# Second expert's first product by seven block products, and the first expert cut at 576 and 240 rows

## Chip, cores and metric

One core of one Trainium2 chip. The metric is the device time of one execution in microseconds; lower is better. Three runs of the kernel before took 835.76, 841.76 and 845.5 us, median 841.76.

## What is computed

A block-sparse attention (4 sequences of 768 rows, 8 heads of 64) feeds a mixture of 8 experts. Each of the 3072 rows of 512 numbers goes to its two best experts; the part that matters here is the second half:

```
logits = x @ w_gate
noisy_logits = logits + np.log1p(np.exp(x @ w_noise)) * noise
top2 = np.argpartition(-noisy_logits, 2, axis=1)[:, :2]
...
for e in range(E):
    for k in range(2):
        mask = top2[:, k] == e
        h = np.maximum(x[mask] @ w1[e], 0.0)          # 512 -> 1024
        out[mask] += top2_w[mask, k, None] * (h @ w2[e])   # 1024 -> 512
```

## The kernel before

**Stages.** The attention runs first, in steps. Behind it a router (class `Router`) handles the rows in four groups of 768: a row's logits, its two experts, its place in each expert's list, and a table `tab` of row numbers and weights, built on TensorE from one-hot matrices in two halves per group (L758) and added up by VectorE (L761). The last group's routing runs beside the first expert's work.

**Units.** The experts are worked as nine units (`Experts.units`, L780). Expert 0 has two: unit 0 holds its rows of the first three groups, up to `CA` = 640, and unit 1 its rows of the last group, up to `CB` = 224. So unit 0 can start before the last routing is done. Units 2 to 8 are experts 1 to 7 with up to `C` = 816 rows each. Rows over these limits go to a slow loop behind the kernel (`overflow`).

**One unit.** GpSimd gathers the rows from DRAM into `xg` (`gather`, L978; a block of 128 rows each), SyncE's queue transposes them into `xta` or `xtb` (`xpose`, L994). The first product (w1) gives 1024 hidden numbers per row in eight groups `f` of 128. Every number is carried as a high and a low half-precision part, so each product is three matmuls. ScalarE writes the high part `hh` of the hidden numbers (`relu`, L1052), VectorE the low part `hl` (L1054). The second product (`mm2`) goes block by block of 128 rows: 24 matmuls of 512 columns (L1160). A remainder of up to 64 rows is done in 12 pairs that sit side by side in the array (L1170), a larger one in transposed form (L1179, then L1191). `finish` weights the rows, and GpSimd scatters them to the output (L1236).

**Plain and fast units.** With `u < FAST` = 3 a unit takes the plain first product: per group 4 x 3 matmuls for each of one or two stretches of rows (`part`, L1040). From unit 3 on it is `fast1`: seven block products in place of eight, each of 6 matmuls of 408 columns (L1079), for each of four pairs of groups. For it the weights are first combined by `sums` (splits L891/L892, sums L911) into the tile `wop`, and the rows by `halves` (L934 on VectorE, L952 on ScalarE) into the tile `tx`; `halves` works in the memory of `xg`, so the next unit's gathers wait for it. The helper `coming` spreads this work over the second product of the unit before.

**Order.** The program is written out in the order of issue and each engine keeps that order. The hooks are: `turn` (up to 20 steps of the router's generator; a step that yields 1 or 2 ends the call, and `FENCE` says how many later calls it then skips), `after(f)` behind each group of a first product, and the loop over blocks of a second product. `third()` is the generator that issues the gathers and transposes of units 1 and 2 once the last routing is done. Its steps are taken behind the blocks of unit 0 and in unit 1.

Of the kernel before, what the change touches and what calls it, by code (L numbers as in the profile page):

```python
# [18 lines left out]
P = 128  # L19
# [8 lines left out]
E = 8  # L28
C = 816
CA = 640  # L30
CB = 224
# [480 lines left out]
class Router:  # L512
# [96 lines left out]
    def run(self, b, ps):  # L609
# [50 lines left out]
        if last:  # L660
            nc.vector.tensor_copy(self.R[:, E:], self.R[:, 0:1])
            nc.vector.memset(self.R[:, 0:1], 0.0)
# [31 lines left out]
        ve = ef  # L694
        if last:
            ve = tile([P, T, 2], F32, "ve")
            nc.vector.scalar_tensor_tensor(ve, z0, float(E), ef, op0=ALU.mult, op1=ALU.add)
        cap = tile([P, T, 2], F32, "cap")
        nc.vector.tensor_scalar(cap, z0, float((CB if last else CA) - C), float(C), op0=ALU.mult, op1=ALU.add)
# [39 lines left out]
        for t in range(0, T, G):  # L739
# [23 lines left out]
            yield  # L763
        if last:
            left = C % P
            w = self.tab.rearrange("p (u c) v -> p u c v", c=NC)[:, 1:E, NC - 1, 1]
            nc.vector.tensor_copy(w[P // 2:P // 2 + left], w[0:left])


class Experts:  # L770
    def __init__(self, tc, router, w1, w2, out, x_dram, table):
# [10 lines left out]
        self.FAST = 3  # L782
# [25 lines left out]
    def open_rows(self, ctx):  # L808
        self.xp = ctx.enter_context(self.tc.tile_pool(name="mxp", bufs=1))
        self.xg = self.xp.tile([P, 7, 2 * self.D], F16, name="xg")  # L810
        self.nc.gpsimd.memset(self.xg[:, C // P], 0.0)
# [22 lines left out]

    def open_third(self, ctx):
        self.ps_h = [self.ps_h[0]] * 2 + [ctx.enter_context(self.tc.tile_pool(name="ps_h3", bufs=1, space=PSUM))]

# [26 lines left out]
    def open_first(self, e):  # L864
        KB, F = self.KB, self.F
        n = KB * F
        if e == 0:
            h, l = (self.wpa.tile([P, n], F16, name=x) for x in ("w1ha", "w1la"))
        else:
            both = self.sums_tile()  # L870
            h, l = both[:, 0:n], both[:, n:2 * n]
        view = lambda t: t.rearrange("p (k f) -> p k f", k=KB)
        self.wb[e] = {"w1h": view(h), "w1l": view(l)}
# [115 lines left out]
    def xpose(self, u, c):  # L989
        r = self.st["u", u]  # L990
        if c == 0:
# [202 lines left out]
    def finish(self, u, c, py, halves=False):  # L1194
# [6 lines left out]
        if u < 2:  # L1201
            nc.vector.tensor_scalar(y[0:m], py[0:m, 0:D], w[0:m, c:c + 1], None, op0=ALU.mult)
        elif u < len(self.units) - 1:
# [122 lines left out]
def count_overflow(nc, router, ps):  # L1326
# [5 lines left out]
    for sl, cap in ((slice(0, 1), CB), (slice(1, E), C), (slice(E, NV), CA)):  # L1332
# [9 lines left out]
def kernel(ctx, tc, q, k, v, v_windows, sampled_blocks, w_gate, w_noise, noise, w1, w2, out):  # L1342
# [154 lines left out]
    def third():  # L1497
# [7 lines left out]
        yield  # L1505
        for i in range(ex.count(1)):
            ex.xpose(1, i)
        for i in range(ex.count(1)):
            ex.gather(2, i)
        yield  # L1510
        for i in range(ex.count(2)):
            ex.xpose(2, i)
        yield

    def coming(u, k):
        e = ex.units[u][1]
        if u + 1 < ex.FAST:
            return
# [25 lines left out]
    for u in range(nu):  # L1544
        if u == 2:
            turns.close()
            ex.open_third(hidden)
        if u == ex.FAST:
# [8 lines left out]
        def after(f):  # L1557
# [7 lines left out]
            if u == 2 and f < 4:  # L1565
                ex.split_piece(e, 4 + f)
# [122 lines left out]
```

## Time and profile before

| what | value |
|---|---|
| median of three runs | 841.76 us |
| profiled execution | 835.04 us |
| its span, first to last instruction | 833.2 us |
| TensorE (PE) busy | 778.8 us, 93% |
| VectorE (DVE), ScalarE (ACT), GpSimd (POOL) busy | 523.5, 391.8, 365.9 us |

Stretches of the span, us from its start, cut where TensorE goes from one product to the next: attention to 301.5; unit 0 first product 301.5 to 333.0, second 333.0 to 360.4; unit 1 360.4 to 380.5; unit 2 first product 380.5 to 413.5, second to 447.5; unit 3 first product 447.5 to 476.5. Matmul rows overlap in time, since their ends are modelled; the time from one start to the next is what a matmul costs. In brackets a row shows how long its engine had stood idle and what ended that.

### The profile page before, as it was taken

To read this page: it belongs to the slowest core of one execution; us is meant where nothing else is said; L and a number is where in the kernel's file an instruction comes from. 1 tells how busy PE (TensorE), PEld (TensorE's weight loads), DVE (VectorE), ACT (ScalarE), POOL (GpSimd) and SP (SyncE) were. 2 spreads that over 40 slices of the span, in tenths; PEclk is the share of its full clock that TensorE was granted. 3 is DMA by queue.
4 is the path that set the end of the run, shared out by engine and by line. 5 is a ranking of instruction groups with operands and counts; after the bars stand their busy time and mean duration, and the time that the engine had idled before them with its cause. 6 is when DMAs were issued, how large, how long until landed. Compare 5 with 4: busy or idle time off the path is not lost. (4 is left out here: it accounts for less than half of the span.)

```text
span 833.2 us, 21747 instructions
## 1 busy us (share of the span) xinstructions
PE 778.8 (93%) x8889; PEld 475.5 (57%) x8889; DVE 523.5 (63%) x1024; ACT 391.8 (47%) x742; POOL 365.9 (44%) x552
## 2 busy tenths in 40 slices
PE   5899988988997898999999999999999999999996
PEld 3577767766676676475545545545545545545542
DVE  4454457557466557423376796796777787886831
ACT  4677666655674652212235445445445445445400
POOL 3465554430364500334055454555447547546521
PEclk9999998999999989999999999999999999999999
DMA  8968987881569789395944984984994894794311
GB/s 332 348 201 266 295 258 225 326 279 53 159 200 249 172 242 346 104 215 137 245 97 80 199 253 76 210 242 82 156 237 113 176 248 105 163 259 109 101 55 53
DMA packets 125707, 159.70 MB, mean 192 GB/s; under 512 B 66629, under 2 KB 84037, under 8 KB 125600
## 3 DMA queue, kind: packets, MB, share of 16 engines
q1 hardware_dynamic: 97232, 75.83, 33.6%
q0 software_dynamic: 20016, 57.47, 27.2%
q10 hardware_dynamic: 8352, 24.93, 9.5%
q8 instruction: 72, 1.18, 0.6%
q14 instruction: 35, 0.29, 0.1%
HBM read 117.30 MB, written 27.10 MB: 173 GB/s over the span
## 5 line engine op out<-in xcount | busy, mean ns | idle before, releaser
L1079 PEld LDWEIGHTS <-wop 128*128 128x128 f16 x1008 | 98.6, 98 | 76.7 <-issue 0.5
L1210 POOL DMA_INDIRECT pv<-out_dram,gi x42 | 96.6, 2301 | 96.2 <-ACT pv L1204 48.0
L1160 PEld LDWEIGHTS <-hh 128*128 128x128 f16 x768 | 74.6, 98 | 89.7 <-issue 2.5
L232 PE MATMUL s<-kv,q 64*32 64x192 f32 (+3 forms) x1920 | 86.8, 348 | 13.9 <-DMA kv<-in_k_dram 5.8
L324 ACT ACTIVATE t<-t 128x512 f32<-128x512 f32 (+1 forms) x120 | 63.1, 567 | 73.4 <-PE t L322 64.4
L1236 POOL DMA_INDIRECT out_dram<-pv,mt x42 | 56.9, 1355 | 84.3 <-DMA out_dram<-pv,mt 33.3
L1079 PE MATMUL mb<-tx,wop 128*128 128x408 f16 x432 | 83.5, 336 | 0.2 <-DVE us L1100 0.2
L322 PE MATMUL t<-r_ident,p 128*128 128x128 f32 x448 | 69.6, 295 | 9.4 <-ACT t L324 4.4
L267 DVE TENSOR_REDUCE nm<-s 128x4 f32<-128x1024 f32 (+1 forms) x48 | 54.3, 1131 | 36.2 <-PE s L232 20.8
L222 POOL COPY kv<-kv 128x128 f32 x264 | 69.6, 308 | 15.5 <-DMA kv<-in_k_dram 9.3
L1160 PE MATMUL py<-w2h,hh 128*128 128x512 f16 x192 | 72.8, 379 | 0.0
L1160 PE MATMUL py<-w1ha,hh 128*128 128x512 f16 x192 | 72.8, 379 | 0.0
L1160 PE MATMUL py<-w2l,hh 128*128 128x512 f16 x192 | 72.8, 379 | 0.0
L1160 PE MATMUL py<-w1la,hh 128*128 128x512 f16 x192 | 72.8, 379 | 0.0
L322 PEld LDWEIGHTS t<-r_ident,p 128*128 128x128 f32 x448 | 50.0, 146 | 35.9 <-issue 15.7
L310 ACT ACTIVATE p<-s,nb 128x256 f32<-128x256 f32 x176 | 69.4, 474 | 1.6
L978 POOL DMA_INDIRECT xg<-x_rows,gi x56 | 61.3, 1094 | 19.5 <-issue 15.9
L1160 PE MATMUL py<-w1ha,hl 128*128 128x512 f16 x192 | 68.9, 379 | 0.0
L1160 PE MATMUL py<-w2h,hl 128*128 128x512 f16 x192 | 68.8, 379 | 0.0
L1084 ACT ACTIVATE hh<-us 128x408 f16<-128x408 f32 x48 | 26.1, 543 | 89.1 <-DVE us L1100 82.5
L232 PEld LDWEIGHTS s<-kv,q 64*32 64x32 f32 (+2 forms) x1920 | 49.2, 126 | 30.4 <-issue 12.6
L1160 PEld LDWEIGHTS <-hl 128*128 128x128 f16 x384 | 37.6, 98 | 45.3
(214 smaller groups left out, 1457.9 us busy)
## 6 DMA issues: line engine op xcount, KB each, us to landing
wraw<-in_moe_w_dram SPq DMA_DIRECT2D x62, 512.0 KB
vb<-in_v_windows_dram ACTq DMA_DIRECT2D x28, 390.0 KB
vb<-in_v_windows_dram ACTq DMA_DIRECT2D x14, 520.0 KB
kv<-in_v_dram SPq DMA_DIRECT2D x4, 1560.0 KB
out_dram<-zero ACTq DMA_DIRECT2D x8, 768.0 KB
q<-in_q_dram SPq DMA_DIRECT2D x11, 512.0 KB
kv<-in_k_dram SPq DMA_DIRECT2D x7, 768.0 KB
x_rows<-x SPq DMA_DIRECT2D x20, 256.0 KB
```

The costliest lines, as they stand in the source:

```text
L222: nc.gpsimd.tensor_copy(KG[:, j, :, 32 * s:32 * s + 32], KT[:, :, bass.ds(offs[3 * j + s], 32)])
L232: mm = lambda out, l, r, pos: nc.tensor.matmul(out, l, r, start=True, stop=True, tile_position=pos)
L267: red = lambda out, x: nc.vector.tensor_reduce(out, x, axis=AX.X, op=ALU.max, negate=True)
L310: self.nc.scalar.activation(p[:, 256 * u:256 * u + 256], S[:, a, 256 * r:256 * r + 256], AF.Exp, bias=nb[:, u:u + 1], scale=0.125)
L322: self.nc.tensor.transpose(T[i][:, c:c + P], p[:, i * w + c:i * w + c + P], self.ident)
L324: self.nc.scalar.activation(t[:, i * w:(i + 1) * w], T[i][:, 0:w], AF.Copy)
L978: g = nc.gpsimd.indirect_dma_start(out=self.xg[0:m, c], out_offset=None, in_=self.x_dram[0:nr], in_offset=bass.IndirectOffsetOnAxis(ap=r[" ...
L1079: self.nc.tensor.matmul(bank[:, 0:H], w[:, h, o, k, cs], x(k, a), start=start and i == 0, stop=i == len(seq) - 1, skip_group_check=True)
L1084: self.nc.scalar.activation(self.hh[:, f, o], x, AF.Relu)
L1160: nc.tensor.matmul(py, h[:, f, o], w[x][:, f, :], start=i == 0, stop=i == last)
L1210: g = nc.gpsimd.indirect_dma_start(out=y[0:m], out_offset=None, in_=self.out, in_offset=bass.IndirectOffsetOnAxis(ap=r["gi"][0:m, c:c + 1] ...
L1236: x = self.nc.gpsimd.indirect_dma_start(out=self.out, out_offset=bass.IndirectOffsetOnAxis(ap=self.st["u", u]["mt"][0:m, c:c + 1], axis=0) ...
```

## The change

Four things. Unit 2 (expert 1) moves from the plain first product to `fast1` (`FAST` 3 to 2); its combined weights are made beside unit 0's second product, its combined rows beside unit 1. Expert 0 is cut at 576 and 240 rows, and rows of the first three groups beyond 576 are passed on to unit 1: for that, five small VectorE instructions join each of the first three routings. Unit 0 then ends in a remainder of 64 rows, done in pairs. The second half of the last table sum goes from the middle of unit 0's second product to the end of its first, and the gathers and transposes of units 1 and 2 are issued from the middle of the first block on. With the reference's inputs expert 0 has 575 rows in the first three groups and 202 in the last.

```diff
-CA = 640
-CB = 224
+CA = 576
+CB = C - CA
...
         cap = tile([P, T, 2], F32, "cap")
-        nc.vector.tensor_scalar(cap, z0, float((CB if last else CA) - C), float(C), op0=ALU.mult, op1=ALU.add)
+        if not last:
+            nc.vector.scalar_tensor_tensor(z0, pos, float(CA), z0, op0=ALU.is_ge, op1=ALU.mult)
+            more = cap[:, 0, 0:1]
+            nc.vector.tensor_reduce(more, z0.rearrange("p t k -> p (t k)"), axis=AX.X, op=ALU.add)
+            yield
+            nc.vector.scalar_tensor_tensor(pos, z0, float(-CA), pos, op0=ALU.mult, op1=ALU.add)
+            nc.vector.tensor_tensor(self.R[:, E:], self.R[:, E:], more, op=ALU.add)
+            yield
+        ve = tile([P, T, 2], F32, "ve")
+        nc.vector.scalar_tensor_tensor(ve, z0, float(E), ef, op0=ALU.mult, op1=ALU.add)
+        nc.vector.tensor_scalar(cap, z0, float(CB - C), float(C), op0=ALU.mult, op1=ALU.add)
...
-        self.FAST = 3
+        self.FAST = 2
...
+            if u == 1:
+                for i in {5: (0,), 6: (1,), 7: (2, 3)}.get(f, ()):
+                    ex.halves(2, i)
-            if u == 2 and f < 4:
-                ex.split_piece(e, 4 + f)
+            if u == 2 and f % 2 == 0:
+                ex.split_piece(e, 4 + f // 2)
...
-                    ex.mm1_first(f, (lambda: turn_rows(NS + 200), lambda: new_logits(NS + 300))[f] if f < 2 else None)
+                    if f == ex.FB - 1:
+                        FENCE[:] = [1, 1]
+                    ex.mm1_first(f, {0: lambda: turn_rows(NS + 200), 1: lambda: new_logits(NS + 300),
+                                     ex.FB - 1: turn}.get(f))
...
+        parts = [(s, i) for s in range(2) for i in range(4)]
+        def mixes():
+            if len(parts) == 8:
+                ex.sums_open(1)
+            ex.sums(1, *parts.pop(0))
+        def halfway():
+            nonlocal rest
+            turn()
+            if u > 0:
+                return
+            if not jobs and rest is None:
+                rest = third()
+                next(rest)
+            mixes()
         for k, c in enumerate(ex.chunks(u)):
-            ex.mm2(u, c, turn)
+            ex.mm2(u, c, halfway)
...
                 if k < 4:
-                    ex.split_piece(1, k)
+                    mixes()
...
-            if u == 1:
-                for _ in range(3):
-                    next(rest, None)
+            if u == 1 and k == 0:
...
+                for i in range(4, 6):
+                    ex.halves(2, i)
```

How the instructions stand on two engines. First TensorE at the seam of unit 0's two products; `r_val` and `r_hot` are the one-hot matrices of the last table. Before, the second half of the table stands inside the second product:

```order
L1160 MATMUL py<-w2h,hh 128x512
L1160 LDWEIGHTS hh
L1160 MATMUL py<-w2l,hh 128x512
L1160 LDWEIGHTS hl
L1160 MATMUL py<-w2h,hl 128x512
L758 MATMUL pr<-r_val,r_hot 128x126 x6
```

and with the change between the last matmul of the first product and the first of the second:

```order
L1040 LDWEIGHTS w1la
L1040 MATMUL ph<-xta,w1la 128x288
L763 MATMUL pr<-r_val,r_hot 128x126 x6
L1160 LDWEIGHTS hh
L1160 MATMUL py<-w2h,hh 128x512
```

It moved ahead by some 36 matmuls of the second product. Next VectorE in unit 1. Before, the eight low parts stand together, and unit 2's plain product follows:

```order
L1054 SCALAR_TENSOR_TENSOR hl<-ph,hh 128x224 x8
L960 TENSOR_SCALAR mt<-r_tab 128x7
L966 TENSOR_SCALAR gi<-mt 128x7
L1202 TENSOR_SCALAR y<-py,r_tab 128x512
L1202 TENSOR_SCALAR y<-pr,r_tab 96x512
L1054 SCALAR_TENSOR_TENSOR hl<-ph,hh 128x816
```

With the change the combined rows of unit 2 (`xg<-xta`, `xg<-xg`, `tx<-xg`) stand between them and before unit 1's results:

```order
L1054 SCALAR_TENSOR_TENSOR hl<-ph,hh 128x240 x6
L934 TENSOR_TENSOR xg<-xta 128x1632
L1054 SCALAR_TENSOR_TENSOR hl<-ph,hh 128x240
L934 TENSOR_TENSOR xg<-xta 128x1632
L1054 SCALAR_TENSOR_TENSOR hl<-ph,hh 128x240
L934 TENSOR_TENSOR xg<-xg 128x2x408 x4
L934 TENSOR_TENSOR tx<-xg,tx 128x1632 x2
L960 TENSOR_SCALAR mt<-r_tab 128x7
L966 TENSOR_SCALAR gi<-mt 128x7
L1202 TENSOR_SCALAR y<-py,r_tab 128x512
L1202 TENSOR_SCALAR y<-pr,r_tab 112x512
L1100 TENSOR_TENSOR r_xT<-mb,um 128x408
```

The seventh and the eighth low part now each stand behind one combining instruction, and six more stand ahead of unit 1's two results.

## Rows read from the trace of the kernel before

**Rows 1.** Windows, one product or unit each: length, each engine's busy time, PEclk, DMA.
```profile
301.50:333.00 31.50, 29.35 (x226) 21.76 (x226) 20.01 (x73) 10.87 (x17) 0.00 (x0) 1.00 0.91 317
333.00:360.40 27.40, 27.37 (x133) 13.05 (x131) 11.85 (x20) 4.49 (x5) 11.83 (x11) 1.00 0.52 113
360.40:380.50 20.10, 19.01 (x221) 16.19 (x222) 4.48 (x12) 3.35 (x9) 3.03 (x3) 1.00 0.87 221
380.50:413.50 33.00, 33.00 (x194) 18.74 (x192) 12.86 (x13) 9.73 (x11) 9.45 (x9) 1.00 0.84 181
...
447.50:476.50 29.00, 29.00 (x167) 16.24 (x166) 21.03 (x36) 12.31 (x22) 13.87 (x13) 1.00 0.74 146
```

**Rows 2.** Timeline of TensorE in unit 0's first product: start, us, instruction.
```profile
309.32 0.71 PE L1040 MATMUL ph<-xta,w1ha 128*128 128x320 f16 x4
...
310.14 0.71 PE L1040 MATMUL ph<-xta,w1ha 128*128 128x320 f16 x4
...
320.89 0.70 PE L1040 MATMUL ph<-xta,w1ha 128*128 128x320 f16 x4 [1.46 <-DVE hl L1054]
...
328.27 1.60 PE L758 MATMUL pr<-r_val,r_hot 128*128 128x126 f32 x12 [0.70 <-DVE r_val L752]
```

**Rows 3.** Timeline of VectorE: a small routing instruction, unit 0's routing, unit 1.
```profile
255.38 0.16 DVE L699 TENSOR_SCALAR r_cap<-r_z 128x12 f32<-128x12 f32 x1
...
320.02 0.82 DVE L1054 SCALAR_TENSOR_TENSOR hl<-ph,hh 128x640 f16<-128x640 f32 x1
...
327.67 0.55 DVE L752 TENSOR_TENSOR r_val<-r_eq,r_pay 128x378 f32<-128x378 f32 x1
...
334.65 0.28 DVE L761 TENSOR_TENSOR r_tab<-r_tab,pr 128x126 f32<-128x126 f32 x1
...
336.64 0.55 DVE L752 TENSOR_TENSOR r_val<-r_eq,r_pay 128x378 f32<-128x378 f32 x1
...
365.53 0.39 DVE L1054 SCALAR_TENSOR_TENSOR hl<-ph,hh 128x224 f16<-128x224 f32 x1 [0.76 <-ACT hh L1052]
```

**Rows 4.** Timeline of TensorE: unit 1's first product, then unit 2's paired remainder.
```profile
361.49 0.35 PE L1040 MATMUL ph<-xtb,w1ha 128*128 128x224 f16 x2 [1.12 <-DMA xtb<-xg]
...
361.77 0.35 PE L1040 MATMUL ph<-xtb,w1ha 128*128 128x224 f16 x2
...
362.06 0.35 PE L1040 MATMUL ph<-xtb,w1ha 128*128 128x224 f16 x2
...
418.87 0.40 PE L1170 MATMUL py<-w1ha,hh 128*48 128x512 f16 x2
419.11 0.38 PE L1170 MATMUL py<-w1la,hh 128*48 128x512 f16 x2
```

**Rows 5.** Timeline of GpSimd: the first gather of unit 1, and one of unit 4.
```profile
347.21 1.67 POOL L978 DMA_INDIRECT xg<-x_rows,gi  x1 [0.30 <-DVE gi L966]
...
463.64 1.32 POOL L978 DMA_INDIRECT xg<-x_rows,gi  x1 [0.30 <-issue]
```

**Rows 6.** Timeline of SyncE's queue: the transposes of units 1 and 2.
```profile
351.34 2.92 SPq L994 DMA_TRANSPOSE xtb<-xg  x2
...
365.38 10.74 SPq L994 DMA_TRANSPOSE xta<-xg  x7
```

**Rows 7.** Groups of instructions of the whole span: busy us, mean ns of one, idle time before.
```profile
L1210 POOL DMA_INDIRECT pv<-out_dram,gi x42 | 96.6, 2301 | 96.2 <-ACT pv L1204 48.0 <-DVE pv L1209 18.6 <-issue 14.1
...
L892 DVE SCALAR_TENSOR_TENSOR wop<-wraw,wop 128x1024 f16<-128x1024 f32 x40 | 48.7, 1218 | 9.5 <-ACT wop L891 9.5
...
L934 DVE TENSOR_TENSOR xg<-xg 128x816 f32<-128x816 f32 x24 | 24.1, 1004 | 0.4
...
L934 DVE TENSOR_TENSOR tx<-xg,tx 128x1632 f16<-128x1632 f32 x12 | 22.3, 1857 | 12.2 <-ACT tx L952 12.2
...
L952 ACT ACTIVATE tx<-xg 128x1632 f16<-128x1632 f32 x12 | 18.6, 1554 | 0.0
...
L934 DVE TENSOR_TENSOR xg<-xta 128x1632 f32<-128x1632 f16 x6 | 11.1, 1851 | 3.9 <-DMA xta<-xg 3.7
```

More of the change, by code (lines that the diff above doesn't have):

```diff
@@ L763, in run @@
             yield
+        w = self.tab.rearrange("p (u c) v -> p u c v", c=NC)
+        if b == self.B - 2:
+            c, left = divmod(CA, P)
+            nc.vector.tensor_copy(w[P // 2:P // 2 + left, 0:1, c, 1], w[0:left, 0:1, c, 1])
         if last:
             left = C % P
-            w = self.tab.rearrange("p (u c) v -> p u c v", c=NC)[:, 1:E, NC - 1, 1]
+            w = w[:, 1:E, NC - 1, 1]
             nc.vector.tensor_copy(w[P // 2:P // 2 + left], w[0:left])
@@ L810, in open_rows @@
         self.xg = self.xp.tile([P, 7, 2 * self.D], F16, name="xg")
-        self.nc.gpsimd.memset(self.xg[:, C // P], 0.0)
+        for c in (CA // P, C // P):
+            self.nc.gpsimd.memset(self.xg[:, c], 0.0)
     def open_right(self, ctx):
@@ L864, in open_first @@
     def open_first(self, e):
[L865 to L872, printed above, removed]
+        h, l = (self.wpa.tile([P, self.KB * self.F], F16, name=x) for x in ("w1ha", "w1la"))
+        view = lambda t: t.rearrange("p (k f) -> p k f", k=self.KB)
         self.wb[e] = {"w1h": view(h), "w1l": view(l)}
@@ L990, in xpose @@
         r = self.st["u", u]
-        if c == 0:
+        if "xt" not in r:
             pool, x = (self.xta, "a") if u % 2 == 0 else (self.xtb, "b")
@@ L1202, in finish @@
             nc.vector.tensor_scalar(y[0:m], py[0:m, 0:D], w[0:m, c:c + 1], None, op0=ALU.mult)
+            if halves:
+                nc.vector.scalar_tensor_tensor(y[0:m], py[H:H + m, 0:D], w[H:H + m, c:c + 1], y[0:m],
+                                               op0=ALU.mult, op1=ALU.add)
         elif u < len(self.units) - 1:
@@ L1331, in count_overflow @@
     ex = pool.tile([P, NV], F32, name="o_ex")
-    for sl, cap in ((slice(0, 1), CB), (slice(1, E), C), (slice(E, NV), CA)):
+    for sl, cap in ((slice(0, 1), CB), (slice(1, E), C), (slice(E, NV), BIGIDX)):
         nc.vector.tensor_scalar(ex[:, sl], pc[:, sl], float(-cap), 0.0, op0=ALU.add, op1=ALU.max)
@@ L1504, in third @@
             ex.gather(2, i)
-        yield
         for i in range(ex.count(1)):
             ex.xpose(1, i)
+        yield
         for i in range(ex.count(1)):
@@ L1511, in third @@
         for i in range(ex.count(2)):
-            ex.xpose(2, i)
+            ex.xpose(2, (i + ex.count(1)) % ex.count(2))
         yield
@@ L1516, in coming @@
         e = ex.units[u][1]
-        if u + 1 < ex.FAST:
-            return
         if k == 0:
@@ L1615 @@
                     next(rest, None)
+                if k == n - 1:
+                    for _ in rest:
+                        pass
                 if k < 4:
-                    ex.split_piece(1, k)
+                    mixes()
+                if k < 2:
                     ex.load_piece(1, 4 + k)
-            if u == 1:
-                for _ in range(3):
-                    next(rest, None)
+            if u == 1 and k == 0:
+                for i in range(6, 8):
+                    ex.load_piece(1, i)
+                for i in range(4, 6):
+                    ex.halves(2, i)
             if nn:
```

11 lines of the change are left out of this document (1 added, 10 removed).

## Prediction

> **What bounds the kernel now.** I read the page first, whose busy shares stand in the table above: TensorE 93%, the next engine 63%. Then the windows, one product each, since the edit touches four of them [rows 1]. From 333 us on TensorE fills its windows (27.37 of 27.40 us, 33.00 of 33.00) at a granted clock of 1.00. There a saving counts in full when it takes columns off TensorE, and a delay counts only if TensorE waits for it. Unit 0's first product is different: 29.35 us busy in 31.50. Its timeline shows two stops, 1.46 us for a low part `hl` and 0.70 us for `r_val` [rows 2]. Both end a chain on VectorE and ScalarE, the last group's routing, which the edit does not shorten. A third stop, of 1.12 us, comes at the start of unit 1, for transposed rows [rows 4]. VectorE's rows [rows 3], the gathers [rows 5], the transposes [rows 6] and the groups [rows 7] then say when the moved work can be ready.
>
> **The change part by part.**
>
> *Price of a matmul.* Six matmuls of 320 columns take 310.14 - 309.32 = 0.82 us, 0.1358 each by the longer run of such rows [rows 2]; three of 224 columns take 0.29, 0.0967 each [rows 4]. That is 0.0391 for 96 columns, 0.0065 for 16.
>
> *Unit 0, first product.* 192 matmuls go from 320 to 288 columns: 192 x 0.0130 = -2.5 us. The stops grow, because the routing chain keeps its length. At group 5 TensorE arrives 1.6 us earlier (120 matmuls), while `hl` of group 3, which ended at 320.84 [rows 3], comes only about 1.25 earlier: its chain starts 0.5 earlier with the last logits and gains some tenths from three shorter low parts. So 1.46 becomes 1.8: +0.35. The first table sum waits for `r_val`, which ended at 328.22 [rows 3] and comes 1.2 earlier; TensorE, held at group 5 and then 48 x 0.0130 = 0.6 faster, waits 1.5 in place of 0.70: +0.8. Bounds for the two together: 0 if the chain moves with TensorE, +1.6 if it does not move at all. I take +1.15, since nearly all of the chain is small VectorE instructions that stay.
>
> *The moved table sum.* Its 12 matmuls (1.6 us by the row of the first half [rows 2]) are only moved: 0. It could stop TensorE at the end of the first product, but `r_val` of the second half was finished 2.5 us after its table add began (334.65 to 337.19 [rows 3]), and one group of 24 matmuls now takes 2.95 us. Counted from the first sum's end at about 328.5, `r_val` is ready at 331.2 and TensorE comes at 331.65. Bounds 0 to +2.5; I take 0. In time before, the first product now ends with the sum at 333.1.
>
> *Unit 0, second product.* Its window holds 120 matmuls and the table's second half: (27.37 - 1.5) / 120 = 0.216 each [rows 1]. Five blocks of 24 become four and 12 pairs. A pair also starts every 0.215 us or so (0.24 in the rows shown, the first of its stretch) [rows 4]. So 12 x 0.216 = -2.6 us. VectorE gets the combined weights here: six splits of 1.22 us [rows 7] and ten instructions over half as many elements, which I put at 0.7, so 14 us in a stretch of 23 with 4 us of other work. TensorE hides it, as only `finish` must follow it, with two result banks of slack. If that cover were gone it would cost up to the few microseconds by which VectorE ran over; I take 0.
>
> *Unit 1's rows.* Before, the first gather stood at 347.21 behind the late table add [rows 5]. Its transposes were issued from 351.34 [rows 6], and TensorE got them at 361.49: 14.3 us in all [rows 4]. Now the add can go at 333.1, the first gather at 334.0, so the rows land at about 348.3, and unit 1 starts at 333.1 + 108 x 0.216 = 356.4. The stop goes: -1.1. Late next are unit 2's rows. Their nine gathers and transposes share the queues: seven behind one another from 334, at up to 1.32 us and a gap of 0.30 [rows 5], end by 345.3; the first two blocks of `xg` are gathered again when unit 1's transposes have read them, by 350, and may need until 356 to land. Seven transposes took 10.7 us to issue [rows 6]. I put the last at about 360 to 363.
>
> *Unit 1, columns.* 96 matmuls of 240 in place of 224 and 96 of 112 in place of 96: 2 x 96 x 0.0065 = +1.25.
>
> *Unit 1, the new order on VectorE.* The first combining instruction takes 1.85 us [rows 7] and stands ahead of the seventh low part, a second one ahead of the eighth. TensorE ends the sixth group at 356.4 + 6 x 12 x 0.1032 = 363.8. A low part ends about 1.0 behind its group (third group's matmuls end at 364.95, its low part at 365.92 [rows 3]), so 364.8. Then 1.85, 0.4, 1.85 and 0.4: the eighth low part is there at 369.3. TensorE ends the first product at 366.3 and wants that part at the 23rd of the next 24 matmuls of 0.049 us: 367.4. It waits +1.9. Bounds: 0 if the combining is late by so much that nothing of this counts (it then costs more below), +4 if both low parts wait. Queued behind are six combining instructions, the table numbers of unit 3 and unit 1's two results.
>
> *Start of unit 2.* TensorE leaves unit 1 at 366.3 + 1.9 + 96 x 0.049 + 24 x 0.216 + 0.4 = 378.5, and after six plain matmuls (1.0) wants the second half of `tx`. VectorE: 369.3, four of 1.0 [rows 7], 373.3; ScalarE writes two high parts of 1.55 from 373.5 on, VectorE two low parts of 1.86 behind them, the last ends at 378.8. That is 0.7 to spare. One more bank is freed only by unit 1's second result, behind `tx`: +0.3 (0 to 2).
>
> *Unit 2, first product.* The plain one took 33.0 us and unit 3's fast one 29.0 for the same rows [rows 1]: -4.0. VectorE was busy 21.03 of 29.00 there with three weight splits; here it has four, 1.2 more, still room.
>
> *Attention.* Five small instructions a group, three groups: 15 x 0.2 (0.16 plus the gap to the next [rows 3]) = 3.0 us on VectorE. The last one's maximum and table instructions also change places. Most lies beside TensorE; bounds 0 to +3.0, I take +0.5.
>
> Sum: -2.5 + 1.15 - 2.6 - 1.1 + 1.25 + 1.9 + 0.3 - 4.0 + 0.5 = -5.1 us. The profiled execution took 835.04 (833.2 of span, 1.84 around it), so 829.9. That execution is the fastest of the times at hand; the median of the three runs is 841.76, 6.7 higher, and 836.7 is my forecast for the median.
>
> **A rule against it.** Gathers ran beside a busy VectorE already: while it was 21 of 29 us busy, the longest of unit 4's seven gathers took 1.32 us [rows 1, 5]. The accumulating ones took 2.30 [rows 7]. The Trainium skill, page "SBUF — State Buffer", section "Who interferes with whom", says that a VectorE instruction with two SBUF inputs contends with a GpSimd instruction that reads SBUF, and that the loser waits for the whole instruction. The splits and sums that now run beside the gathers of units 1 and 2 are such instructions; by this rule each of the nine gathers could be held by one of up to 1.22 us, and the rows of unit 2 would come up to 11 us later, as in rival B. The plain gathers' rows speak against it, the accumulating ones' do not exclude it.
>
> **The rivals.**
>
> *No new stop (A).* The routing chain moves with TensorE, the low parts come in time, the attention hides its three microseconds: -2.5 - 2.6 - 1.1 + 1.25 - 4.0 = -8.95, 832.8 on the median. For it: TensorE stood still for under 4 us in all of 301 to 413. Against it: the order on VectorE, which is fixed, and 1.85 us per combining instruction.
>
> *Unit 2's rows come late (B).* Unit 1's two transposes, beside gathers, took from 351.34 to 361.4, or 5.0 us each [rows 4, 6], where unit 2's seven were issued at 1.5 each with no gathers beside them. Now these seven run beside gathers too. The third gather starts at 337.2 and lands like unit 1's first after 4.1 (347.21 to 351.34 [rows 5, 6]): from 341.3, at 5.0 each, the last is there at 376.3. VectorE wants it at 364.8, and all of unit 1's end moves by 11.5: +6.4, 848.2, slower than before. The sign turns where the last transpose lands behind 369.9, at 4.1 each; gathers held on GpSimd would come to the same. For it: the DMA engines were 0.87 busy in unit 1 [rows 1]. Against it: the long one of the two holds mostly the time to land, not a rate, and there are 13 us of head start.
>
> *The attention pays (C).* All 3.0 us on the path: -2.6, 839.2. For it: the routing holds TensorE at the table sums, as at 328.27 [rows 2]. Against it: VectorE is 63% busy over the span, so most of its instructions have room around them.
>
> *The slow loop.* If expert 0 overflowed 576 + 240 rows, the loop behind the kernel would run; 575 and 202 rows exclude it.
>
> **How the numbers follow.** Forecast 0.52, A 0.18, B 0.13 (with the skill's rule), C 0.17. One per cent, about what a measurement of this kernel can tell from no change, is 8.4 us: faster means under 833.3. That is most of A and the part of the forecast's spread in which one of its stops is missing: 0.25. Slower, above 850.2, needs B and a little more: 0.05. Within 1%: 0.70. The range runs from 829 (A with the spread of the runs shown, some 4 us) to 846: C and most of B.
>
> **What would show it.** Right: unit 2's first product at 29 us with `mb<-tx` matmuls; no wait for `xtb` at unit 1's start; a stop of about 2 us in L1179 for `hl`; a stop of 1.5 at the first table sum and none at the second. Wrong: a stop on `tx` or on DMA `xta` at unit 2's start, gathers over 2 us, a first table sum in unit 0 that waits as before, or an attention that ends later than 301.5 by over 1 us.

## The result and the profile after

The changed kernel took 849.73 us at the median of 22 executions (839.92 to 859.75), the kernel before 840.63 beside it. The ratio is 1.0077, with a 95% interval of 1.0049 to 1.0105: slower, where 836.7 us and no change worth telling were forecast; 849.73 also lies above the range of 829 to 846. (The ratio leaves out executions over 1.5% above the fastest of their kernel, six of the 22 after and two before; the two medians by themselves give 1.0108.) Two later measurements of the same program gave 1.0002 (0.9943 to 1.0061) and 1.0056 (1.0019 to 1.0094). The profiled execution took 852.05 us, 17.0 over the one before (835.04).

Windows of the changed kernel, one product each (unit 1 whole) and then the units 3 to 7; columns as in [rows 1]:

```profile
302.10:333.36 31.26, 29.36 (x237) 23.71 (x236) 22.26 (x78) 11.70 (x19) 0.00 (x0) 0.95 0.84 299
333.36:356.89 23.53, 23.53 (x122) 10.60 (x120) 14.66 (x23) 5.67 (x7) 12.86 (x10) 1.00 0.92 181
356.89:388.71 31.82, 22.03 (x221) 17.66 (x220) 20.33 (x26) 7.25 (x12) 4.39 (x5) 0.89 0.64 138
388.71:416.67 27.96, 27.39 (x156) 15.24 (x156) 17.86 (x30) 11.64 (x21) 10.90 (x10) 1.00 0.83 193
416.67:453.10 36.43, 36.11 (x181) 16.35 (x180) 31.00 (x37) 17.84 (x22) 19.22 (x10) 1.00 0.54 130
453.10:780.00 326.90, 317.29 (x1682) 158.74 (x1681) 243.91 (x333) 144.12 (x210) 168.47 (x109) 0.99 0.76 166
```

Unit 0 did what was forecast: its second product is 23.53 us long with no gap. The loss begins in the third row. Unit 1 is 31.82 us long (20.10 in [rows 1]), and TensorE is busy for only 22.03 of it, at a granted clock of 0.89. Unit 2's first product is 5 us shorter. In the last row TensorE is idle for 9.6 us in units that the edit does not touch.

Timeline of TensorE in the changed kernel, the answers to [rows 2] and [rows 4]:

```profile
320.20 0.65 PE L1040 MATMUL ph<-xta,w1ha 128*128 128x288 f16 x4 [1.91 <-DVE hl L1054]
...
332.02 1.50 PE L763 MATMUL pr<-r_val,r_hot 128*128 128x126 f32 x12
...
365.90 0.56 PE L1040 MATMUL ph<-xtb,w1ha 128*128 128x240 f16 x2 [6.39 <-DVE hl L1054]
...
377.57 0.21 PE L1179 MATMUL py<-hl,w2h 128*128 128x112 f16 x1 [1.68 <-DVE hl L1054]
...
388.71 1.02 PE L1079 MATMUL ma<-xta,wop 128*128 128x408 f16 x5 [1.73 <-DVE y L1202]
```

The largest stop, 6.39 us, stands inside unit 1's first product, for a low part `hl`. No such stop was in the forecast. Why `hl` is late stands in VectorE's timeline:

```profile
347.56 0.75 DVE L1202 TENSOR_SCALAR y<-py,r_tab 128x512 f32<-128x512 f32 x1
...
359.13 0.75 DVE L1202 TENSOR_SCALAR y<-py,r_tab 128x512 f32<-128x512 f32 x1 [6.01 <-DMA out_dram<-y,mt]
...
364.78 0.75 DVE L1202 TENSOR_SCALAR y<-py,r_tab 128x512 f32<-128x512 f32 x1 [0.57 <-DMA out_dram<-y,mt]
365.45 0.71 DVE L1054 SCALAR_TENSOR_TENSOR hl<-ph,hh 128x240 f16<-128x240 f32 x2
```

VectorE writes a block's result into one of three buffers `y` (the pool has three). The fourth result, unit 0's next to last block, has to wait until the first block's scatter has left its buffer. That costs 6.01 us. VectorE keeps its order, so weight splits and unit 1's first low parts queue up behind. Why the scatter is late stands in GpSimd's timeline and SyncE's queue:

```profile
334.71 2.03 POOL L978 DMA_INDIRECT xg<-x_rows,gi  x1 [44.13 <-DVE gi L966]
...
344.43 0.93 POOL L978 DMA_INDIRECT xg<-x_rows,gi  x1 [0.30 <-issue]
345.67 1.04 POOL L1239 DMA_INDIRECT out_dram<-y,mt  x1 [0.30 <-issue]
347.01 1.43 POOL L978 DMA_INDIRECT xg<-x_rows,gi  x1 [0.30 <-issue]
...
359.82 0.96 POOL L1239 DMA_INDIRECT out_dram<-y,mt  x1 [9.50 <-issue]
```

```profile
339.23 3.03 SPq L994 DMA_TRANSPOSE xtb<-xg  x2
...
343.07 22.75 SPq L994 DMA_TRANSPOSE xta<-xg  x7
```

The first scatter is issued at 345.67, behind the seven gathers that the change put ahead of it. It is done at 359.0, 13.4 us later. In the kernel before, the first two scatters had no gathers ahead of them and took 2.9 and 2.7 us (340.02 to 342.9, 345.90 to 348.6). Here the data come in the order of issue, the seventh gather's at 356.7 and then the scatter's, and they share the DMA engines with the transposes. Seven transposes of unit 2 now take 22.75 us to issue, where they took 10.74 in [rows 6].

Where the time went, by unit. Each number is the time between the first matmuls of two units in the profiled execution (the last column to the end), us:

| execution | unit 0 begins | unit 0 | unit 1 | unit 2 | units 3 to 8 |
|---|---|---|---|---|---|
| before | 301.6 | 59.9 | 19.0 | 67.0 | 385.7 |
| before, again (e1) | 304.8 | 58.6 | 19.5 | 67.0 | 385.0 |
| after | 302.0 | 54.9 | 31.8 | 64.4 | 397.1 |
| after, again (e5) | 306.6 | 54.9 | 30.5 | 64.4 | 384.8 |
| after, third (e11) | 297.6 | 54.7 | 31.6 | 64.4 | 385.0 |

Two things are to be explained: unit 1, 11 to 13 us longer in all three, and the units 3 to 8, 11 us longer in one of three. That a unit from 3 on takes longer than its usual 62.9 us, with stops of TensorE for ScalarE, is called a slip below.

### The profile page after: what moved, and what is told of

Read it like the earlier page. It is cut to its first block, busy times and chain, and to the rows that moved or that the text cites. A ratio compares the mean times of both kernels' runs of the same rounds, so it can differ in the third digit from the quotient of the medians.

```text
span 850.2 us, 21805 instructions
## 1 busy us (share of the span) xinstructions
PE 776.5 (91%) x8865; PEld 473.8 (56%) x8865; DVE 556.6 (65%) x1088; ACT 400.6 (47%) x760; POOL 374.1 (44%) x554
## 3 DMA queue, kind: packets, MB, share of 16 engines
q0 software_dynamic: 19984, 57.37, 27.8%
## 5 line engine op out<-in xcount | busy, mean ns | idle before, releaser
L1079 PEld LDWEIGHTS <-wop 128*128 128x128 f16 x1176 | 115.0, 98 | 92.5 <-issue 4.1
L1213 POOL DMA_INDIRECT pv<-out_dram,gi x42 | 101.0, 2405 | 94.6 <-ACT pv L1207 27.1
L1160 PEld LDWEIGHTS <-hh 128*128 128x128 f16 x752 | 73.3, 98 | 99.2 <-issue 15.2
L1079 PE MATMUL mb<-tx,wop 128*128 128x408 f16 x504 | 97.7, 336 | 1.0 <-DVE us L1100 0.9
L978 POOL DMA_INDIRECT xg<-x_rows,gi x56 | 64.4, 1151 | 60.9 <-DVE gi L966 44.8
L891 ACT ACTIVATE wop<-wraw 128x1024 f16<-128x1024 f32 x42 | 44.1, 1053 | 85.1 <-DVE wraw L911 55.2
L1084 ACT ACTIVATE hh<-us 128x408 f16<-128x408 f32 x56 | 30.4, 543 | 102.7 <-DVE us L1100 96.2
L1160 PE MATMUL py<-w2h,hh 128*128 128x512 f16 x184 | 70.7, 384 | 7.1 <-ACT yt L1207 7.1
L1160 PE MATMUL py<-w1ha,hh 128*128 128x512 f16 x192 | 72.8, 379 | 2.5 <-ACT yt L1207 2.5
L1160 PE MATMUL py<-w1la,hh 128*128 128x512 f16 x192 | 72.8, 379 | 0.0
L1160 PE MATMUL py<-w2l,hh 128*128 128x512 f16 x184 | 70.5, 383 | 0.0
L1160 PE MATMUL py<-w1ha,hl 128*128 128x512 f16 x192 | 68.9, 379 | 0.0
L232 PEld LDWEIGHTS s<-kv,q 64*32 64x32 f32 (+2 forms) x1920 | 49.2, 126 | 32.8 <-issue 13.6
L1160 PE MATMUL py<-w2h,hl 128*128 128x512 f16 x184 | 66.8, 383 | 0.0
```

The lines of the kernel that those rows point to most:

```text
L232: mm = lambda out, l, r, pos: nc.tensor.matmul(out, l, r, start=True, stop=True, tile_position=pos)
L891: self.nc.scalar.activation(hi, t, AF.Copy, scale=scale)
L978: g = nc.gpsimd.indirect_dma_start(out=self.xg[0:m, c], out_offset=None, in_=self.x_dram[0:nr], in_offset=bass.IndirectOffsetOnAxis(ap=r[" ...
L1079: self.nc.tensor.matmul(bank[:, 0:H], w[:, h, o, k, cs], x(k, a), start=start and i == 0, stop=i == len(seq) - 1, skip_group_check=True)
L1160: nc.tensor.matmul(py, h[:, f, o], w[x][:, f, :], start=i == 0, stop=i == last)
L1213: g = nc.gpsimd.indirect_dma_start(out=y[0:m], out_offset=None, in_=self.out, in_offset=bass.IndirectOffsetOnAxis(ap=r["gi"][0:m, c:c + 1] ...
```

## The experiments

Twelve runs. Ratios are against runs of the kernel before on the same chip. The theories have their letters from the expectations.

**e1, the kernel before again** (an empty line added), one execution.

> The kernel before once more, for a second profile of it. In the changed kernel's profile units 3 to 8 lose 11.4 us that the first profile of before does not lose. Theory P (the change also slows the later units): here every unit from 3 on again takes 62.9 us with no stop of TensorE over 1 us, whatever the total. Rival Q (these stops come and go in any execution, and the first profile of before was a lucky one at 835 where the median is 841): here one or more units take 64 us and more, with waits for ACT yt at the second product.

Measured: 836.73 us, no unit from 3 on over 63.2 us. So the kernel before shows no late slip in two profiles.

**e2, results of units 0 and 1 in another buffer.**

```diff
-        y = self.pv[:, c] if 2 <= u < len(self.units) - 1 else self.yp.tile([P, D], F32, name="y")
+        y = self.pv[:, c + 5 * (u == 1)] if u < len(self.units) - 1 else self.yp.tile([P, D], F32, name="y")
```

> The changed kernel, with the results of units 0 and 1 written to the tile pv (a place of its own for each block) in place of three buffers taken in turn; nothing else differs. Theory Y (the buffers): VectorE stood 6.0 us at 353.1 for the scatter of the first block to land, and TensorE 6.4 us at unit 1's third group behind it. Both are gone here, unit 1 ends 6 us earlier, time about 6 us under the changed kernel, near 1.000 of before. Rival R (the rows): without that stop VectorE reaches the first combining instruction of unit 2 at about 365, but unit 2's transposes, whose last was issued at 365.8, land later: VectorE then waits there for xta and unit 1 ends at most 3 us earlier; ratio 1.004 or more.

Measured: ratio 1.0026 (0.9972 to 1.0080). The stop of 6.39 us is gone, and unit 1 takes 27.3 us in place of 31.8: the `y` buffers were its cause. The 4.5 us lie between the theories, 6 by Y and at most 3 by R, and R's wait for `xta` is there too. What comes next stands in the timeline of e2, VectorE and TensorE:

```profile
371.56 1.86 DVE L934 TENSOR_TENSOR xg<-xta 128x1632 f32<-128x1632 f16 x1 [1.83 <-DMA xta<-xg]
373.34 0.40 DVE L1054 SCALAR_TENSOR_TENSOR hl<-ph,hh 128x240 f16<-128x240 f32 x1
373.65 1.85 DVE L934 TENSOR_TENSOR xg<-xta 128x1632 f32<-128x1632 f16 x1
375.42 0.40 DVE L1054 SCALAR_TENSOR_TENSOR hl<-ph,hh 128x240 f16<-128x240 f32 x1
...
373.79 0.21 PE L1179 MATMUL py<-hl,w2h 128*128 128x112 f16 x1 [1.51 <-DVE hl L1054]
375.87 0.21 PE L1179 MATMUL py<-hl,w2h 128*128 128x112 f16 x1 [1.77 <-DVE hl L1054]
```

VectorE waits 1.83 us for unit 2's rows and then holds both last low parts behind a combining instruction each, and TensorE stops twice for them. In this execution the units 6 and 7 took 67.9 and 68.1 us.

**e3, the cut at 576 and 240 rows alone** (with the passing-on in the routing; no early table sum, no block product in unit 2).

```diff
-CA = 640
-CB = 224
+CA = 576
+CB = C - CA
...
```

> The kernel before with the cut at 576 and 240 rows alone (the router's five small instructions, the remainder of 64 rows in pairs); expert 1 stays plain, and the last table sum and the gathers stay where they were. Theory F (the loss comes with the fast unit 2 and its place): columns save 3.9 us, the routing stops cost 1.2, the stop at unit 1's start grows from 1.1 to 4 or 5, since the gathers come no earlier: no change, ratio 0.996 to 1.002, and no new stop in unit 1 behind its start. Rival G (the cut and its router cost): the attention ends over 1 us later than 301.5 and the ratio is 1.003 or more.

Measured: ratio 1.0042 (0.9996 to 1.0087). Unit 0 takes 59.6 us and unit 1 21.8, with a stop of 4.43 us for DMA `xtb<-xg` at its start. A shorter unit 0 is worth nothing while the rows of unit 1 come no earlier: the cut needs the early table sum. The stop is as theory F had it, but the ratio is over its 0.996 to 1.002, and both of rival G's numbers came (unit 0 began at 305.9). Yet up to unit 3 this profile is 2.5 us longer than that of before and 3.2 longer than e1's, most of the 3.5 us that the ratio gives, so G's cost in the attention is not shown.

**e4, the cut and the early table sum, with the early gathers and transposes**; unit 2 plain.

```diff
...
-            ex.mm2(u, c, turn)
+            ex.mm2(u, c, halfway)
...
+                if k == n - 1:
+                    for _ in rest:
+                        pass
```

> As e3, with the last table sum at the end of the first product and the gathers and transposes of units 1 and 2 issued from the middle of the first block on, as in the changed kernel; expert 1 still plain. Theory F: unit 1's start has no stop, 4 us faster than before, ratio about 0.995. Rival Y as it bears here: the first block's scatter again stands behind seven gathers, its buffer comes free at about 359, VectorE stops for 6 us with less work of its own in the queue, and TensorE stops in unit 1 for 3 us or more; ratio about 1.000.

Measured: ratio 1.0046 (1.0013 to 1.0079). Unit 0 falls to 54.7 us, unit 1 rises to 27.8, with a stop of 4.77 us for `hl`; this is theory Y's stop, though the ratio is above both theories' numbers. VectorE stood idle for 7.15 us before its fourth result, which began at 359.09 when the first scatter was done at 359.0, and for 2.84 before the fifth, for DMA `out_dram<-y`. So the wait for `y` belongs to the early gathers, and needs no block product.

**e5, the changed kernel again.**

> The changed kernel again, unedited but for an empty line. Theory P (the 7 us that the units 4 to 8 lost come from the block product of unit 2: GpSimd's chain of adding gathers, scatters and gathers has no room for a unit that is 4 us shorter, and a chain that is late once stays late): the units 3 to 8 are again 6 to 12 us longer in all than in the kernel before, with the stops in L1160. Theory Q (chance of that one execution): their lengths are within 2 us of before's (62.9 each), and the profiled time is 7 to 10 us under the first profile's. Either way the stop of 6.4 us at unit 1's start and that of 1.7 us at unit 2's first bank return.

Measured: ratio 1.0002 (0.9943 to 1.0061). A stop of 4.03 us in unit 1, 1.68 in L1179 and 1.73 at unit 2's first bank, as at first; the units 3 to 7 at 62.9 us each. Theory P, in the form that the slip comes every time, falls.

**e6, e4 with the buffers of e2**: the cut and the early sum, unit 2 plain, no wait for `y`.

> The kernel of the fourth run (576/240 rows, early sum of the table, unit 2 still by plain products) with the results of units 0 and 1 in the pv buffer in place of the three y buffers. Theory Y: the stop of 4.8 us in unit 1 falls to under 1.5 us and the time by 3 to 4 us against that run's ratio of 1.0046, to 0.998 to 1.001. Theory P: no slip in the units 3 to 8 (62.9 us each), since unit 2 is not shortened; with it the difference to the second run, which is the same but for the block product in unit 2, is that product alone. Theory Q: the slip of 10 us can come here as well.

Measured: ratio 0.9988 (0.9952 to 1.0023), profiled 830.78 us. Unit 1 takes 20.2 us, unit 2 67.2, the units 3 to 7 62.9 each. No stop over 0.3 us is left behind unit 0's first product. Both theories' numbers came, Y's in full. With e2, which takes 91.7 us for the units 1 and 2, it tells the price of the block product in this order of VectorE's work: 87.4 us without it.

**e7, e2 with the next expert's first four weight pieces loaded earlier**, two ahead of the transposes and two between them.

```diff
+                if f == 0:
+                    ex.load_piece(e + 1, 0)
+                    ex.load_piece(e + 1, 2)
+                if f == 2:
+                    ex.load_piece(e + 1, 1)
+                    ex.load_piece(e + 1, 3)
...
```

> The second run's kernel (changed kernel, results of units 0 and 1 in pv) with the loads of the next expert's first four weight pieces issued ahead of the transposes on SyncE's queue (in the groups 0 and 2 of a first product instead of 5 and 6). Theory P: the slip reaches TensorE through these loads, which stand behind the transposes and so behind late gathers; with them ahead the stops in L1160 go, the units 3 to 7 are 62.9 to 63.5 us each, and the time is 8 to 10 us under the second run's: ratio 0.986 to 0.993. Rival W: it is the gathers and transposes themselves (rows late for the combining instructions), not the loads: the stops stay, ratio 1.000 to 1.004; or the loads' 2 MB beside the gathers makes these later still, ratio over 1.004.

Measured: ratio 1.0160 (1.0098 to 1.0221), units up to 72.3 us, stops of 6.69, 4.91 and 2.52 us in L1160. The rival's numbers came, theory P's did not. In unit 4 the seven transposes took 25.5 us with two loads between them, where seven took 15.9 in e6. So this order is no remedy: with loads among them the transposes came later still. It does not clear the loads, since the last four of the eight pieces still stand behind the transposes.

**e8, e2 with the transposes of unit 1's small block in the middle of its last block.**

```diff
+            if u == 1 and c == 0:
+                ex.turn(1, 1)
...
-            if left_ and k == min(2, n - 1):
+            if left_ and u != 1 and k == min(2, n - 1):
```

> The second run's kernel with the transposes of unit 1's 112-row block put in the middle of its last block's product instead of behind it. Theory B (the first bank of unit 2 waits for VectorE's read of that block's transposes): the stop of 1.73 us at unit 2's start falls to under 0.5 us. Rival: the last block's own result is read as late, and 1 us or more stays. By theory P the units 3 to 8 slip again by 8 to 12 us, so that the ratio is 0.999 to 1.004; by theory Q they do not, and it is 0.988 to 0.993.

Measured: ratio 0.9971 (0.9935 to 1.0007); the profiled execution was its slowest, 858.17 us, with the units 4 to 7 at 65.4 to 68.5. The stop at unit 2's first bank fell from 1.73 to 1.07, so the rival had the larger part: the last block's own result is late too. The spread of its executions, 830 to 858 us, makes its ratio a weak witness on the slip.

**e9, e8 with another order on VectorE in unit 1.**

```diff
-            if d == 0:
+            if "tx" not in r:
...
-                for i in {5: (0,), 6: (1,), 7: (2, 3)}.get(f, ()):
+                for i in {7: (0, 1, 2, 3)}.get(f, ()):
...
-                for i in range(4, 6):
+            if u == 1 and k == 1:
+                for i in (5, 4):
+                    ex.halves(2, i)
```

> The eighth run's kernel (results of units 0 and 1 in pv, transposes of unit 1's small block in the middle of its last block's product) with VectorE's order in unit 1 changed: all low parts of the eight groups first, then the combining instructions, then the two results, then the low halves of the combined rows, d = 1 ahead of d = 0 as the product needs them. Theory O (the block product of unit 2 loses in unit 1, by VectorE's order, more than it gives back in unit 2): the stops in L1179 (3.0 and 1.6 us) go, one stop of 1 to 2 us comes at the first mixed product of unit 2, units 1 and 2 together take 87 to 89 us (92.7 in the eighth run, 87.4 in the sixth with the plain product), ratio 0.990 to 0.996 unless the units 3 to 8 slip. Rival V: VectorE's work in unit 1 is the bound in whatever order: as long a stop stands at unit 2's start and the two units still take 91 to 93 us.

Windows of e9 (units 1 and 2) and, below them, of e8 (the same two units, kernel and profile of that run):

```profile
359.30:379.30 20.00, 20.00 (x221) 16.75 (x220) 13.26 (x19) 5.04 (x11) 3.90 (x5) 1.00 0.72 184
379.30:446.00 66.70, 63.84 (x338) 31.60 (x337) 53.05 (x70) 30.86 (x44) 30.15 (x20) 1.00 0.67 152
```

```profile
361.30:389.60 28.30, 22.60 (x222) 18.92 (x221) 16.93 (x22) 6.42 (x11) 4.72 (x4) 0.88 0.65 161
389.60:454.00 64.40, 63.51 (x337) 31.60 (x337) 49.42 (x68) 29.48 (x42) 30.72 (x19) 1.00 0.67 154
```

Unit 1 is full again, at clock 1.00, and the stops moved to unit 2's first mixed products (1.40 and 0.57 us, for `tx`): 86.9 us for both, from first matmul to first matmul, in place of 92.7. Theory O holds for these units: the order on VectorE cost 5.8 us. But the gain is small even so, 86.9 against 87.4 in e6. The ratio, 0.9996 (0.9958 to 1.0033), misses the 0.990 to 0.996; in the profile the units 6 and 7 slipped, to 65.0 and 68.2.

**e10, e6 again; e11, the changed kernel a third time.**

> The sixth run's kernel again (plain product in unit 2). Theory P2 (the later units slip in more executions when unit 2 is shortened): no slip here, the units 3 to 7 are 62.8 to 63.2 us each, the times of its executions spread over less than those of the ninth and eleventh run. Theory Q (a slip by chance in either): 2 us or more in those units can come here too. Ratio 0.995 to 1.000 as in the sixth run.

> The changed kernel a third time, with rounds enough for an interval beside the two others. By the stages of the first two profiles it loses 5 us up to unit 3 by itself, so 1.003 to 1.008 with slips in some executions, and 0.998 to 1.003 without; a profile with the units 3 to 7 at 62.9 us each speaks for Q, one with 65 us or more in several of them for P2.

Measured: e10 0.9907 (0.9866 to 0.9948), units 1 and 2 in 87.2 us, no slip. e11 1.0056 (1.0019 to 1.0094), a stop of 4.89 us in unit 1, no slip in its profile, which its expectation counts for Q. Leaving e7 and e12 aside, kernels with the block product in unit 2 slipped in four of six profiles (after, e2, e8, e9), those with the plain one in none of six (before, e1, e3, e4, e6, e10: no unit from 3 to 7 over 64.4 us, and that one, in e4, has a stop for VectorE). And e9 and e10 are level up to unit 3, 141.7 and 142.1 us from unit 0's start, while e9's median is 5.9 us above e10's. That speaks for P2; it does not say why. But P2's other sign did not come: the executions of e10 spread over 22.9 us (823.8 to 846.7), those of e9 over 13.8 and those of e11 over 19.3. And e6 and e10, the same kernel, came out at 0.9988 and 0.9907 with intervals that do not touch, so a difference of 0.8% between two measurements is weak by itself.

**e12, e6 with GpSimd late once**: twelve clearings of a block in place of one, ahead of unit 5's gathers.

```diff
-                nc.gpsimd.memset(ex.xg[:, C // P, 0:8 * C - 12 * ex.D], 0.0)
+                for _ in range(12 if u == 3 else 1):
+                    nc.gpsimd.memset(ex.xg[:, C // P, 0:8 * C - 12 * ex.D], 0.0)
```

> The sixth run's kernel (plain product in unit 2, which showed no slip in two profiles) with GpSimd's clearing of the rows' last block repeated twelve times, once, ahead of unit 5's gathers, so that these start some 5 us later in unit 4 (at 15 to 16 us in it in place of 11) and all later ones find the chain late. Theory S (a chain that is late once stays late, its transposes then run beside the scatters, and TensorE pays in every later unit): last transposes of the units 4 to 7 at 33 us or later, stops in L1160, these units 65 to 68 us, time 8 to 12 us over the sixth run's, ratio 1.00 to 1.01. Theory U (lateness alone is absorbed, and the slip needs what else the block product of unit 2 changes): gathers at 14 us or later, but the units 62.8 to 63.5 us, ratio 0.990 to 0.999 as in the sixth and tenth run.

Windows of e12, the units 4 to 7, and of e6, the units 4 to 6:

```profile
511.20:577.20 66.00, 63.04 (x338) 31.63 (x337) 47.69 (x67) 28.29 (x42) 36.51 (x33) 1.00 0.68 160
577.20:641.90 64.70, 63.01 (x338) 31.59 (x337) 48.81 (x68) 28.86 (x43) 34.51 (x23) 1.00 0.75 169
641.90:709.90 68.00, 64.88 (x338) 32.07 (x337) 50.26 (x69) 29.48 (x43) 35.42 (x23) 0.97 0.76 165
709.90:772.80 62.90, 62.90 (x338) 31.69 (x337) 48.98 (x66) 28.87 (x42) 37.46 (x23) 1.00 0.72 178
```

```profile
506.90:569.70 62.80, 62.80 (x338) 31.55 (x337) 49.06 (x68) 28.98 (x42) 33.11 (x22) 1.00 0.77 175
569.70:632.60 62.90, 62.90 (x338) 31.69 (x337) 49.11 (x68) 28.87 (x42) 31.65 (x22) 1.00 0.78 175
632.60:695.50 62.90, 62.90 (x338) 31.69 (x337) 49.11 (x68) 28.88 (x42) 30.37 (x22) 1.00 0.73 175
```

The timeline of e12 in unit 4 (GpSimd, SyncE's queue, ScalarE, TensorE), and below it that of e6:

```profile
523.61 5.67 POOL L1656 MEMSET xg<- 128x384 f16 x12
529.61 1.06 POOL L988 DMA_INDIRECT xg<-x_rows,gi  x1 [0.33 <-issue]
...
533.12 15.47 SPq L1004 DMA_TRANSPOSE xtb<-xg  x7
548.69 5.21 SPq L867 DMA_DIRECT2D wraw<-in_moe_w_dram  x6
...
554.04 1.06 ACT L901 ACTIVATE wop<-wraw 128x1024 f16<-128x1024 f32 x1 [7.84 <-DMA wraw<-in_moe_w_dram]
...
556.42 0.38 PE L1170 MATMUL py<-w1ha,hh 128*128 128x512 f16 x1 [2.96 <-ACT yt L1217]
```

```profile
517.71 1.06 POOL L988 DMA_INDIRECT xg<-x_rows,gi  x1 [0.16 <-issue]
...
521.21 15.94 SPq L1004 DMA_TRANSPOSE xtb<-xg  x7
537.25 3.42 SPq L867 DMA_DIRECT2D wraw<-in_moe_w_dram  x5
```

One delay of 5.2 us, in a kernel without the block product in unit 2, makes three units longer: 66.0, 64.7 and 68.0 us, until unit 7 runs at 62.9 again. Theory S's lengths came in two units, 64.7 lies just under them, and the last unit escaped, so a late chain does not stay late for good. The gathers start 18.4 us into unit 4 (529.61 less 511.2) where they started 10.8 into it in e6 (517.71 less 506.9); 5.2 of these 7.6 us are the clearings, the rest had come on GpSimd before. The transposes are as fast, but the weights behind them are loaded from 37.5 us on, not 30.4. ScalarE waits 7.84 us for a weight piece with TensorE's results `yt` queued behind it, and TensorE stops. The ratio is 1.0053 (1.0020 to 1.0087), against 0.9988 and 0.9907 without the delay. So gathers as late as this are enough for the slip, without the block product.

The same chain stands in the changed kernel's first profile, unit 5 (from 580.0): SyncE's queue, ScalarE, TensorE.

```profile
602.09 17.70 SPq L994 DMA_TRANSPOSE xta<-xg  x7
619.90 17.60 SPq L863 DMA_DIRECT2D wraw<-in_moe_w_dram  x8
...
624.94 1.06 ACT L891 ACTIVATE wop<-wraw 128x1024 f16<-128x1024 f32 x1 [9.97 <-DMA wraw<-in_moe_w_dram]
...
627.31 0.59 PE L1160 MATMUL py<-w2h,hh 128*128 128x512 f16 x1 [5.08 <-ACT yt L1207]
```

**What TensorE pays for is when the weights are loaded.** The units 3 to 7 of all profiles but e7's, whose loads stand elsewhere, are 65 units. In 15 of them the first weight load behind the transposes is issued 36.2 us or later after the unit's first matmul: each of these has a stop of 0.9 to 5.1 us for ScalarE and takes 1.0 to 7.3 us more than 62.9. In the 50 others it is issued at 35.2 us or before, and none has such a stop. Late gathers alone do not bring it. SyncE's queue in unit 7 of the kernel before (from 699.35) and in unit 6 of e2 (from 641.64):

```profile
717.77 13.44 SPq L994 DMA_TRANSPOSE xta<-xg  x7
731.62 17.11 SPq L857 DMA_DIRECT2D wraw<-in_moe_w_dram  x8
```

```profile
659.74 21.07 SPq L994 DMA_TRANSPOSE xtb<-xg  x7
680.92 16.77 SPq L863 DMA_DIRECT2D wraw<-in_moe_w_dram  x8
```

The gathers begin 15.0 and 14.2 us into these units, about alike. The transposes take 13.44 us in the one, the loads begin at 32.3 us and nothing stops; they take 21.07 in the other, the loads begin at 39.3 and the unit takes 67.9 us.

**What stays open.** Two things set when the loads begin, and neither was traced to its cause: when GpSimd comes to the gathers, and how long seven transposes take. Gathers 13.6 us or more into a unit stand in 14 of the 30 units of the six profiles with the block product, and in 4 of 30 in the six with the plain one. From unit 3 on the two programs are the same.

## Why the prediction was wrong, point by point

**The step that failed.** It is the sentence on unit 0's second product: "TensorE hides it, as only `finish` must follow it, with two result banks of slack ... I take 0." `finish` does not only need a bank to read from. It needs a buffer to write to, there are three, and the scatter that frees one stands behind the seven gathers that this change moves ahead of it. I counted the gathers' own way to `xg` and not what they were moved past. Cost: a stop of 6.39 us (4.03 and 4.89 in the other two profiles), and a lower clock behind it. With that wait gone unit 1 is 4.5 us shorter (e2), with the plain product behind it 7.6 us shorter (e6 against e4). In all, -5.6 us were forecast from unit 0's start to unit 3's; measured are +5.2 in the first profile, +3.8 and +4.8 in the other two.

**The order on VectorE in unit 1: mis-sized.** I took +1.9 us for the stop in L1179 and +0.3 for the bank. Measured are 1.68 and 1.73, while the larger stop before covered the rest. Without it the L1179 stops are 3.3 us in e2 and 4.6 in e8, the latter above the bound of +4, and the matmuls slow down besides. Another order on VectorE gave back 5.8 us (e9).

**Unit 2's first product: right, but not all gain.** It fell by 5.0 us, and the unit from 67.0 to 64.4, 2.6 us, where I had 4.0: the second product grew by 2.4, since the last group's 12 block matmuls run inside it. Those were in the 29.00 us that I took from [rows 1], so -4.0 could have held; 0.9 of the missing 1.4 are small stops (27.39 us busy of 27.96, 36.11 of 36.43), the rest I can't place. A shorter unit 2 paid by a longer unit 1 is a loss: 91.7 and 92.7 us for both in e2 and e8, 87.4 in e6.

**The units 3 to 8: missing.** I had 0. They cost 11.4 us in one profile of three, by the slip. The forecast took a saving on TensorE to count in full from 333 us on, since TensorE was full in the windows; that it was full said nothing of how near the next engine's chain was. In e6 the weights are loaded from 30.4 us into unit 4 and nothing stops; from 37.5 us (e12) TensorE does.

**What held.** Unit 1 began at 356.89 in the trace (356.4 forecast). The stop at `hl` was 1.91 us (1.8), and none came at the second table sum. The wait for `xtb` went. The seven gathers were issued by 345.4 (345.3). So the -2.5, -2.6, -1.1, +1.15 and 0 for the moved sum together were right: unit 0 is 5.0 us shorter. The +1.15 came in part by luck. At the first table sum, where 1.5 us were forecast, the stop was 1.3 us in e4, e7, e8, e11 and e12, and under 0.3 here and in the other six. In the five the granted clock of the first product was 1.00, in these seven 0.94 to 0.95, with a stretch at the lower level behind the stop for `hl`: TensorE lost there what it did not wait later. Nearly all signs that the prediction had named as right came, and the loss was in a place that no sign watched.

**The rivals.** B in its own form did not come: in e2 unit 2's rows were there 10.2 us after unit 1's start (371.56 less 361.34), against 3.6 to 6.6 by the forecast and 19.9 by B. Its reason, transposes beside gathers, was right, at 3.25 us each (22.75 over 7); it struck at the scatter first. C can't be told: unit 0 began between 297.6 and 308.8 us in the twelve profiles with the edited routing, at 301.6 and 304.8 in the two without. A fell with its premise that no new stop comes.

**The rule set against the change.** For plain gathers it did not matter: the longest of the nine took 2.03 us, just over the 2 us named as a sign of being wrong, and all seven were out in time. For the adding gathers it did. Timeline of e8, VectorE and GpSimd, and below it that of e5, at the end of unit 2:

```profile
445.97 1.86 DVE L934 TENSOR_TENSOR tx<-xg,tx 128x1632 f16<-128x1632 f32 x1 [3.08 <-ACT tx L952]
...
446.06 3.22 POOL L1213 DMA_INDIRECT pv<-out_dram,gi  x1 [0.30 <-ACT tx L952]
```

```profile
448.27 1.58 POOL L1214 DMA_INDIRECT pv<-out_dram,gi  x1 [0.30 <-issue]
...
448.37 1.86 DVE L935 TENSOR_TENSOR tx<-xg,tx 128x1632 f16<-128x1632 f32 x1 [3.08 <-ACT tx L953]
```

Begun 0.09 us behind VectorE's `tx`, it takes 3.22 us; begun 0.10 ahead of it, 1.58. The Trainium skill, page "SBUF — State Buffer", section "Who interferes with whom", has the rule, and that the one which comes first keeps the shared ports for the whole instruction; here the trace agrees. The next one in e8 took 3.05, and the gathers in unit 3 then began 12.0 us into it, not 9.4 as in e5. That makes GpSimd later, but it was not shown to bring the slip: e5 has adding gathers of 2.7 to 3.2 us in its units 4 to 7 and no slip.

## What to carry to other kernels

When work is moved ahead of other work on an in-order queue, list what it is moved past, and for each of these who waits for its end: here a scatter frees a buffer, the buffer lets VectorE go on, and VectorE lets TensorE go on. A saving on the busiest engine counts only as far as the next chain has room, so measure that room, in us of lateness, before the saving is summed; full windows don't show it. The version to keep is the cut and the early sum with enough result buffers and the plain product in unit 2: 0.9988 and 0.9907 in two measurements, which is about level with the kernel before or better by 1%.

## What was not expected of the hardware

**A short stop costs more than its length.** Behind the 6.39 us stop the 221 matmul rows of unit 1 have TensorE busy for 22.03 us at a granted clock of 0.89; the same unit without stops (e9) takes 20.00 at 1.00. In e2, whose two stops are of 1.51 and 1.77 us, the 10 us from 371 to 381 ran at a mean clock of 0.83. So part of the time was at the lower of the two levels, 1.2 GHz, after TensorE had stood still.

**A scatter of 256 KB took 13.4 us from its issue to its end** because of what had been issued ahead of it; with no gathers ahead, two took 2.9 and 2.7 us in the kernel before. From 337 to 359 us GpSimd's queue moved 2.2 MB, 0.1 MB per us, with the transposes' packets on the same DMA engines. The Trainium skill, page "DMA: Bandwidth & Descriptors", section "SWDGE vs HWDGE vs iDMA", says that only one queue is allocated to GpSimd's transfers and that a DMA engine takes turns between its queues. The trace agrees: all of GpSimd's packets carry one queue's name, and from 341 to 359 us both this queue and the transposes' are at work in every 2 us; the turns themselves it does not show.
